# Windowed attention and squared-ReLU MLP on one core: the planner's load costs, pacing, Q turns of batch 0 and idle matmuls

## The chip, the cores and the metric

The kernel runs on one core of a Trainium2 chip. Time is device microseconds from start to end of one execution; the figure compared is the median of several runs. A profile of one execution gives every instruction's start and length on the engines: TensorE (PE, with its weight loads as PEld), VectorE (DVE), ScalarE (ACT), GpSimd (POOL) and SyncE (SP). The last two mainly issue DMAs here.

## The reference

```python
# q, k, v: 8 batches, 8 heads, 576 positions, 64 wide; w_in: 512 x 2048, w_out: 2048 x 512
scores = (1.0 / np.sqrt(D)) * np.matmul(q, k.transpose(0, 1, 3, 2))
mask = np.abs(pos[:, None] - pos[None, :]) <= 32
scores = np.where(mask, scores, -1000000000.0)
attn = softmax(scores)                       # over the last axis
x = np.matmul(attn, v).transpose(0, 2, 1, 3).reshape(B * S, H * D)     # 4608 x 512
r = np.maximum(x @ w_in, 0.0)
out = (r * r) @ w_out                        # 4608 x 512, float32
```

Each query sees at most 32 keys on either side. Nearly all arithmetic is in the two dense products.

## The kernel before, in words

**Attention.** A batch is 9 chunks of 64 queries, in all 72 chunks, numbered n. For a chunk, `scores` multiplies 128 keys with 64 queries for the 8 heads (line 565), ScalarE takes the exponential (581), VectorE multiplies with the band mask (588), `av` multiplies with V extended by a column of ones (607, 608), VectorE takes the reciprocal of that column (619) and scales into `xr` (621). `xturn` turns xr into the layout that the dense part needs, `XT`: for chunks below 18 on TensorE with a copy by ScalarE (643, 648), after that by a transposing DMA on SP's queue (631). From batch 2 on (`FB = 2`) three chunks are done together.

**Inputs.** Q, K and V are loaded in pieces by POOL's DMA queue, cast to bf16 on the way (`tok_load`, 452; `vx_load`, 514); only the first two pieces of Q and K of batch 0 come by the queues of SP and ACT (445). Q and K have to be turned: in batches 0 and 1 on TensorE (`tok_turn`, 475), with copies out of PSUM by VectorE (489), or, for Q of the first three pieces, by ScalarE (486); from batch 2 on by transposing DMAs on SP (`dma_turn`, 508). V is needed a second time shifted by 64 rows for odd chunks: VectorE copies it (`vd_half`, 524).

**Dense part.** A tile T is 512 rows of x, so 9 tiles. The first product (W1) of a tile is 16 blocks: four accumulating 128x512 products into one of two PSUM banks `HT` (`mm1`, 700), Relu by ScalarE (706), square by VectorE (715). Tile 0 and half of tile 1 use blocks of 128 rows by four (`mm1_small`, 661), called (group of rows, quarter of w_in) below; the rest of tile 1 uses `mm1_half` (682). The second product (`mm2`, 751) accumulates 16 products for 128 rows of output in one of two banks `OUTP`, then ScalarE copies the result (760) and issues its store (762). w_in and w_out are loaded once, in four quarters each, on POOL's queue (529, 534).

**Order.** The program is not written in the order in which it runs. Every operation is recorded with `rec` together with what it reads and writes, an estimated duration (`dur`) and, for DMAs, an estimate `move`: packets, ns for each, and a further latency. `schedule` plans all engines with these estimates: it plays the program forward with several pads added to each DMA's end (`PADS`), backward to find due times, and forward again with those as priorities; turns and attention (`att`) can be given a margin (`MARGINS`). Each plan's order is judged with random lateness, and the best order is kept. The order on each engine is then fixed and each engine goes through its list, waiting on semaphores where needed. So an engine's queue is strictly in order: what stands behind a waiting instruction waits too.

**Pace.** Loads of batches 2 and later are not issued as early as buffers allow. `pace` makes each load wait for a W1 block, counted in the order in which blocks are recorded:

```python
l = 2 * (9 * b + 1.8 * x + 0.6 * z - PACE)
return [("mo", max(0, int(l)))] if l < 16 * NT else []
```

where b is the batch, x the piece, and z 0, 1 or 2 for K, Q or V.

**Idle matmuls.** `fill` puts products of zeros (`ZZ`, line 405) into the planned gaps of TensorE up to a planned time `WARM` and to the operation `idle_end`, at full density up to the planned time `COLD` and at the density `SPARSE` after it. They write bank `OUTP[1]`.

Of the kernel before, what the change touches and what calls it, by code (L numbers as in the profile page):

```python
# [8 lines left out]
BF16 = mybir.dt.bfloat16  # L9
# [10 lines left out]
VS = D_ + 2  # L20
KW = 32 + S_ + 32
LEAD = 12
WARM, COLD, SPARSE = 36000, 6500, 0.5
NPE = 18
TOFF, TST = 6, 0.9
FB = 2
PACE = 15
ENGS = ("PE", "ACT", "DVE", "POOL", "SP")
PADS, MARGINS, ROUNDS, NREP = (0, 1000, 2000, 4000), (0, 4000, 10000), 3, 3
LATE = {"POOL": 1500, "SP": 2000, "ACT": 2000}  # L30
DEPTH, POST, BACK = 4000, {"POOL": 1500, "SP": 1000, "ACT": 1000}, {"POOL": 2500, "SP": 4000, "ACT": 4000}
ORDER = ("v00 v01 k02 q02 v02 w10 k03 q03 v03 w11 k04 q04 v04 w12 w13 w20 w21 w22 w23 k05 q05 "
# [7 lines left out]

class Op:
    __slots__ = ("eng", "fn", "deps", "order", "inc", "val", "sem", "dma", "dur", "key", "i",
                 "succ", "pred", "start", "end", "lat", "move", "att")


class Prog:
# [13 lines left out]
    def rec(self, eng, fn, reads=(), writes=(), dma=None, dur=100, key=0.0, move=0, old=(), att=False):  # L60
        op = Op()
        op.eng, op.fn, op.dma, op.dur, op.key, op.move = eng, fn, dma, dur, key, move
        op.att = att
        op.deps, op.order = set(), set()
        op.inc, op.val, op.sem = False, None, None
        op.lat = self.LAT[eng]
        for r in reads:
            for w in self.writer.get(r, ()):
                op.deps.add(w)
        for t in writes:  # L70
            for w in self.writer.get(t, ()):
                (op.order if w.eng == eng and w.dma is None and dma is None else op.deps).add(w)
            for r in self.readers.get(t, ()):
                (op.order if r.eng == eng and eng not in ("ACT", "DVE") and r.dma is None else op.deps).add(r)
        for t in old:
            for r in self.readers.get(t, ()):
                (op.order if r.eng == eng and r.dma is None and dma is None else op.deps).add(r)
        for r in reads:
            self.readers.setdefault(r, []).append(op)
        for t in writes:  # L80
            self.writer[t] = [op]
            self.readers[t] = []
        op.i = len(self.ops)
        self.ops.append(op)
        return op
# [10 lines left out]
    def forward(self, key=None, seq=None, rnd=None, pad=0):  # L96
# [29 lines left out]
        def serve(until):  # L126
            nonlocal now, ahead
            while now < until:
# [28 lines left out]
                if sw:  # L157
                    ahead -= x
                if op is not None:
                    end[op.i] = max(now, start[op.i] + op.dur) + POST[op.eng] + (op.move[2] if len(op.move) > 2 else 0) + (rnd.random() * rnd.late[op.eng] if rnd else pad)  # L160
                    done(op, end[op.i])
                    return True
            return False
# [99 lines left out]
    def schedule(self):  # L263
# [22 lines left out]
        for pad in PADS:  # L286
            f = self.forward(key=key, pad=pad)
            keep(f[2], f[0], f[1], f[3], ("keys", pad))
            for margin in MARGINS:
                start, T = f[0], f[3]  # L290
                for k in range(ROUNDS):
                    R = self.backward(start, T)
                    kk = [1e4 * op.key if op.key <= -100 else r - (margin if op.att else 0) for r, op in zip(R, self.ops)]
                    start, end, out, T = self.forward(key=kk, pad=pad)
                    keep(out, start, end, T, (pad, margin, k))
        self.log, self.R = log, R
# [7 lines left out]
    def fill(self, out):  # L304
        at = 1200
        for op in sorted((o for o in out if o.eng == "PE"), key=lambda o: o.start):
            gap = min(op.start, WARM, self.idle_end.start) - at
            one = 215 if at < COLD else 110
            for k in range(int((gap - 100) * (1 if at < COLD else SPARSE) // one)):
                w = Op()  # L310
                w.eng, w.fn, w.dma, w.deps, w.i = "PE", self.idle, None, {self.idle_on}, op.i
                w.inc, w.val, w.sem, w.start, w.end, w.dur, w.key = False, None, None, at + one * k, 0, one, -99
                out.append(w)
            at = max(at, op.start + op.dur)
        self.ops = sorted(out, key=lambda o: (o.start, o.i))
# [41 lines left out]
class Gen:  # L357
# [43 lines left out]
    def setup_idle(self):  # L401

        self.ms("DVE", ["zz"], self.ZZ[:], 0.0, -1000, 200)
        self.p.idle_on = self.p.ops[-1]
        self.p.idle = lambda e: e.matmul(self.OUTP[1][:, 0:256], self.ZZ[:, 0:128], self.ZZ[:, 0:256], start=True, stop=True)

    def setup_masks(self, key):
        self.p.rec("POOL", lambda e: e.iota(self.IOTA[:], [[1, 256]], base=0, channel_multiplier=-1), writes=["iota"],
# [31 lines left out]
    def first_load(self, t, x, eng, key):  # L440
        t0, n = PIECE0[x]
        src = (self.q if t == "q" else self.k)[0, :, t0:t0 + n, :].rearrange("h p d -> p h d")
        stg, tag = self.STG[t, x]
        dst = bass.AP(stg, 0, [[512, n], [64, 8], [1, 64]])
        self.p.rec(eng, lambda e: e.dma_start(dst, src), writes=[tag], dma=(f"s{t}{x}", 0), key=key, dur=420, move=(n // 2, 14, 1300))

    def tok_load(self, b, t, x, key):
        t0, n = self.pieces(b)[x]
# [3 lines left out]
        self.p.rec("POOL", lambda e: e.dma_start(dst, src), writes=[("fraw", b, t, x)], old=[("fraw", b - 2, t, y + (b == 2))],  # L452
                   reads=self.pace(b, x, "kqv".index(t)), dma=(f"f{b % 2}{t}{y}", b), key=key,
                   dur=500 + 3.2 * n, move=(n // 2, 13.3, 700 if b == 0 else 200))

    def tok_turn(self, b, x, key):
        t0, n = self.pieces(b)[x]
# [6 lines left out]
        elif b or x == 5:  # L464
            parts = [("k", "sD", self.TRP[:, 0:512]), ("q", "sD", self.TRP[:, 512:1024])]
        else:
            o = self.OUTP[0][:].bitcast(BF16)
            parts = [("k", ("outp", 0), o[:, 0:512]), ("q", ("outp", 0), o[:, 512:1024])]

        def f(e, todo):  # L470
            for t, tag, ps in todo:
# [6 lines left out]
        for todo in ([parts[:1], parts[1:]] if early else [parts]):  # L478
            rd = [self.STG[t, x][1] for t, _, _ in todo] + [("oe", 3)] if first else [("fraw", b, t, x) for t, _, _ in todo]
            self.p.rec("PE", lambda e, a=todo: f(e, a), reads=rd + ["id"],  # L480
                       writes=list({tag for _, tag, _ in todo}), key=key, dur=8 * n if first else 240 * len(todo), att=True)
        for t, tag, ps in parts:
            src = ps[:, 0:512].rearrange("p (j q) -> p j q", j=4)[:, :, 0:n]
            dst = self.KT[b % 2][:, :, 32 + t0:32 + t0 + n] if t == "k" else self.QT[b % 2][:, :, t0:t0 + n]
            if early and t == "q":
                self.p.rec("ACT", lambda e, d=dst, c=src: e.activation(d, c, ACTF.Copy), reads=[tag], writes=[(t, b % 2, x)],
                           old=self.was(b, t, x), key=key, dur=200 + 2.8 * n, att=True)
            else:
# [14 lines left out]
    def dma_turn(self, b, t, x, key):  # L503
# [3 lines left out]
        dst = self.KT[i][:, :, 32 + t0:32 + t0 + n] if t == "k" else self.QT[i][:, :, t0:t0 + n]  # L507
        self.p.rec("SP", lambda e: e.dma_start(dst, src, transpose=True), reads=[("fraw", b, t, x)], writes=[(t, i, x)],
                   old=self.was(b, t, x), dma=(f"t{t}{i}{x}", b), key=key, dur=1250, move=(32, 28 if n > 64 else 20), att=True)

    def vx_load(self, b, s, key):
        t0, n = PIECE[s]
        r = 32 if s == 0 else 0
        self.p.rec("POOL", lambda e: e.dma_start(  # L514
            self.VX[b % 2][r:r + n, s, :, 0:64], self.v[b, :, t0:t0 + n, :].rearrange("h p d -> p h d")),
            writes=[("vxl", b % 2, s), ("vxl", b % 2, s, 1)], reads=self.pace(b, s, 2), dma=(f"vf{b % 2}{s}", b), key=key, dur=500 + 3.2 * n, move=(n // 2, 13.3, 700 if b == 0 else 200))

    def vd_half(self, b, s0, s1, key):
        vd, vx = self.VD[b % 2], self.VX[b % 2]
# [219 lines left out]
    def mm2(self, T, u, seg, key):  # L739
# [9 lines left out]
        def f(e):  # L749
            for d in range(4 * seg, 4 * seg + 4):  # L750
# [2 lines left out]

        self.p.rec("PE", f, reads=[("gt", T % 2, d, u) for d in range(4 * seg, 4 * seg + 4)] + [("w2", seg)],
                   writes=[tag], key=key, dur=854)
        if x == 1 and seg == 0:
            self.p.idle_end = self.p.ops[-1]
        if seg == 3:
            oe = self.OE[x % 4]
            self.p.rec("ACT", lambda e: e.activation(oe[:], op, ACTF.Copy), reads=[tag],  # L760
# [132 lines left out]
```

## Time and profile before

| | |
|---|---|
| median of 5 runs | 311.48 us (311.04 to 312.07) |
| profiled execution | 313.03 us |
| span of its instructions | 311.2 us |
| granted TensorE clock, mean | 0.994 |
| PE busy | 298.3 us, 2801 instructions |
| first mm2 starts | 36.86 us |
| last product ends | about 308.6 us |
| DMA moved | 39.20 MB |

The span runs from the first to the last instruction; the profiled execution has 1.83 us more around it. Busy time of TensorE includes the idle matmuls, and the ends of products are modelled because they overlap: in the dense part a 128x512 product is listed with 379 ns, but four of them follow each other in 864 ns, which is the figure for sums. In a list of waits, a line reads: engine, what waited, then what it waited for, total microseconds, times, and the longest. In a timeline the columns are start, length, engine, line, operation, what is written and read, shape and count; a bracket gives the idle time of the engine ahead of it and what ended that.

### The profile page before, as it was taken

Reading aid. Unit: us, or ns where it says so; the run is one execution under the profiler, and the core shown is the slowest. Engines: PE = TensorE matmul, PEld = TensorE weight load, DVE = VectorE, ACT = ScalarE, POOL = GpSimd, SP = SyncE. Lnnn points to the kernel's source line nnn. Section 1 sums busy time; section 2 is a strip of 40 time slices with the busy share of each in tenths; the row PEclk is TensorE's granted clock in tenths of the full one; section 3 lists DMA queues with packets and bytes.
Section 4 is the critical chain, followed back from the end, with each engine's and each line's share of the span. In section 5 each row is a group of like instructions: output and inputs, shape, how many; then the busy total and the mean of one; then the engine's idle time right before and its main releaser. Section 6 shows DMA issues by size and latency. Waiting matters only on the chain.

```text
span 311.2 us, 7048 instructions
## 1 busy us (share of the span) xinstructions
PE 298.3 (96%) x2801; PEld 166.4 (53%) x2801; DVE 149.3 (48%) x449; ACT 150.3 (48%) x267; POOL 105.4 (34%) x131
## 2 busy tenths in 40 slices
PE   6969999999999999999999999999899999999996
PEld 4658845687754455444545554545354454444444
DVE  6765434664665564744556642745254542222200
ACT  2536533555746554654465544635355533434411
POOL 8999370322505533532442353333421000000000
PEclk9899999999999999999999999999999999999999
DMA  9999999994999999999999999999999420100022
GB/s 132 180 191 207 178 174 175 158 146 97 132 156 123 145 127 166 121 158 130 130 170 154 112 108 202 139 99 147 132 150 137 61 60 34 36 34 35 36 81 87
DMA packets 166098, 39.20 MB, mean 126 GB/s; under 512 B 157233, under 2 KB 161585, under 8 KB 166065
## 3 DMA queue, kind: packets, MB, share of 16 engines
q0 software_dynamic: 114144, 18.03, 90.4%
q1 hardware_dynamic: 45424, 11.09, 25.9%
q10 hardware_dynamic: 6496, 9.64, 9.5%
q8 instruction: 22, 0.36, 0.5%
q14 instruction: 12, 0.09, 0.1%
HBM read 36.70 MB, written 9.44 MB: 148 GB/s over the span
## 4 chain that ended last, share of the span: by engine, by line
PE 77%; DMA 15%; POOL 4%; DVE 1%; issue 1%; ACT 1%; SPq 0%; DVEq 0%; POOLq 0%; ACTq 0%
PE outp L751 31%; PE ht L700 28%; PE ht L661 6%; DMA vx<-in_v_dram 5%; DMA w<-in_moe_w_in_dram 3%; PE sc L565 3%; PE ht L682 2%; PE sc L607 2%; PE sc L608 2%; DMA qt<-qraw 2%; DMA kraw<-in_k_dram 2%; POOL vx L514 2%; DMA xt<-xr 1%; DMA kt<-kraw 1%; POOL qraw L452 1%
## 5 line engine op out<-in xcount | busy, mean ns | idle before, releaser
L751 PE MATMUL outp<-w,gt 128*128 128x512 bf16 x528 | 128.8, 379 | 0.0
L700 PE MATMUL ht<-xt,w 128*128 128x512 bf16 x448 | 110.2, 379 | 0.8 <-DMA xt<-xr 0.8
L706 ACT ACTIVATE rt<-ht 128x512 bf16<-128x512 f32 x112 | 66.8, 599 | 78.9 <-PE ht L700 75.3
L715 DVE TENSOR_TENSOR gt<-rt 128x512 bf16<-128x512 bf16 x144 | 60.8, 422 | 87.4 <-ACT rt L706 76.8
L751 PEld LDWEIGHTS outp<-w,gt 128*128 128x128 bf16 x528 | 49.5, 98 | 55.7
L700 PEld LDWEIGHTS ht<-xt,w 128*128 128x128 bf16 x448 | 41.8, 98 | 48.2 <-DMA xt<-xr 0.9
L452 POOL DMA_DIRECT2D kraw<-in_k_dram x39 | 33.1, 848 | 46.7 <-PE ht L700 18.2
L452 POOL DMA_DIRECT2D qraw<-in_q_dram x39 | 33.0, 847 | 45.9 <-PE ht L700 23.1
L581 ACT ACTIVATE e<-sc 128x512 bf16<-128x512 f32 x72 | 38.7, 600 | 17.6 <-PE sc L565 17.5
L514 POOL DMA_DIRECT2D vx<-in_v_dram x40 | 34.1, 853 | 36.7 <-PE ht L700 14.7
L588 DVE TENSOR_TENSOR pt<-e,mask 128x512 bf16<-128x512 bf16 x72 | 27.2, 421 | 25.1 <-ACT e L581 24.9
L760 ACT ACTIVATE oe<-outp 128x512 f32<-128x512 f32 x33 | 19.8, 599 | 23.9 <-PE outp L751 23.9
L621 DVE TENSOR_TENSOR xr<-sc,rs 128x256 bf16<-128x256 f32 x72 | 28.9, 416 | 1.0
L661 PE MATMUL ht<-xt,w 128*128 128x128 bf16 x384 | 23.8, 219 | 1.7 <-DMA w<-in_moe_w_in_dram 1.7
L524 DVE COPY vd<-vx 64x1056 bf16<-64x1056 bf16 (+1 forms) x36 | 17.5, 486 | 14.7 <-DMA vx<-in_v_dram 13.8
L661 PEld LDWEIGHTS ht<-xt,w 128*128 128x128 bf16 x384 | 21.7, 98 | 2.2 <-DMA w<-in_moe_w_in_dram 2.0
L667 ACT ACTIVATE rt<-ht 128x512 bf16<-128x512 f32 x24 | 14.4, 599 | 14.5 <-PE ht L661 14.4
L619 DVE RECIPROCAL rs<-sc 128x4 f32<-128x4 f32 x72 | 12.6, 179 | 14.6 <-PE sc L608 13.6
L565 PEld LDWEIGHTS sc<-qt,kt 64*128 64x128 bf16 x576 | 10.4, 95 | 11.7 <-issue 7.7
L565 PE MATMUL sc<-qt,kt 64*128 64x64 bf16 x576 | 13.9, 192 | 2.7 <-DMA qt<-qraw 1.6
L607 PE MATMUL sc<-vx,pt 128*128 128x65 bf16 x160 | 15.3, 194 | 0.6 <-DVE pt L588 0.4
L608 PE MATMUL sc<-vx,pt 128*128 128x65 bf16 x160 | 15.2, 194 | 0.0
(69 smaller groups left out, 163.0 us busy)
## 6 DMA issues: line engine op xcount, KB each, us to landing
out_dram<-oe ACTq DMA_DIRECT2D x35, 256.0 KB, 2.8
kraw<-in_k_dram POOLq DMA_DIRECT2D x30, 128.0 KB, 5.8
qraw<-in_q_dram POOLq DMA_DIRECT2D x30, 128.0 KB, 5.2
vx<-in_v_dram POOLq DMA_DIRECT2D x24, 128.0 KB, 5.1
w<-in_moe_w_in_dram POOLq DMA_DIRECT2D x4, 512.0 KB, 10.3
w<-in_moe_w_out_dram POOLq DMA_DIRECT2D x4, 512.0 KB, 17.5
vx<-in_v_dram POOLq DMA_DIRECT2D x16, 96.0 KB, 5.3
kt<-kraw SPq DMA_TRANSPOSE x30, 4.6
```

The source lines that it names most:

```text
L452: self.p.rec("POOL", lambda e: e.dma_start(dst, src), writes=[("fraw", b, t, x)], old=[("fraw", b - 2, t, y + (b == 2))], reads=self.pace( ...
L514: self.p.rec("POOL", lambda e: e.dma_start(self.VX[b % 2][r:r + n, s, :, 0:64], self.v[b, :, t0:t0 + n, :].rearrange("h p d -> p h d")), w ...
L565: mm = e.matmul(sc[:, o + 64 * j:o + 64 * j + 64], kt[r, j, at:at + 128], qt[r, j, at:at + 64], start=True, stop=True)
L581: self.p.rec("ACT", lambda e, d=dst, a=src: e.activation(d, a, ACTF.Exp, scale=0.125), reads=["s" + x for x in name], writes=[("e", g, x) ...
L588: self.p.rec("DVE", lambda e, a=pt, c=ee, d=mb: e.tensor_tensor(a, c, d, ALU.mult), reads=rd + ["mask"], writes=[("pt", (n + k) % 3)], key ...
L607: e.matmul(o, pt[:, a:a + 128], vt[:, ha, 0:VE], start=True, stop=False)
L621: self.p.rec("DVE", lambda e: e.tensor_tensor(bass.AP(xr, 256 * k, [[768, 128], [64, 4], [1, 64]]), bass.AP(self.SC, base, [[2048, 128], [ ...
L661: mm = e.matmul(ht[:, 128 * (d % 4):128 * (d % 4) + 128], self.W1[:, ft, 128 * d:128 * d + 128], self.XT[:, t0 // 64:t0 // 64 + 2, ft, :], ...
L700: mm = e.matmul(ht[:], self.W1[:, ft, 128 * d:128 * d + 128], self.XT[:, 8 * T:8 * T + 8, ft, :], start=(ft == 0), stop=(ft == 3))
L706: self.p.rec("ACT", lambda e: e.activation(rt[:], ht[:], ACTF.Relu), reads=[("ht", k % 2)], writes=[("rt", k % 4)], key=key, dur=560)
L715: self.p.rec("DVE", lambda e: e.tensor_tensor(g, r, r, ALU.mult), reads=[("rt", k % 4)], writes=tags, key=key, dur=430)
L751: mm = e.matmul(op, gt[:, d, 128 * u:128 * u + 128], self.W2[:, d, :], start=(d == 0), stop=(d == 15))
```

## The change

Five things change.

1. The planner's estimates. Latencies of the early loads are larger (`first_load` 1300 becomes 1400, and 2100 for the second piece; V of batch 0 700 becomes 1500, 1100 or 800). A `slack` of 3000 ns is added, in planning only, to the end of each load and each DMA turn of Q and K from batch 2 on. The pad of 4000 and the margin of 10000 are replaced by 2000 as the largest pad and 8000 as the largest margin, margins are given only to operations with a key above `LATER = 4`, and plans are judged on 4 draws instead of 3. The plan kept before was one with a pad of 2000; the plan kept now has a pad and a margin of 0.
2. `PACE` goes from 15 to 17, so each paced load waits for a W1 block that stands four earlier.
3. In batch 0, pieces 3 and 4, K is turned in `OUTP[0]` and Q in `OUTP[1]` instead of both in `OUTP[0]`, and the Q copy out of PSUM goes from VectorE to ScalarE. `idle_end` is now the turn of piece 3, because the idle matmuls write `OUTP[1]`.
4. Idle matmuls have 128 columns instead of 256, are planned at 107 ns (before `COLD`, which goes from 6500 to 9000) or 54 ns instead of 215 or 110, and fill gaps from 60 ns instead of 100.
5. A list made from a set becomes a sorted list.

Because the planner fixes the order of all engines, every engine's order changes, not only the lines named. In the built program, idle matmuls go from 37 in nine places to 56 in six (29, 2, 4, 7, 13, 1), the last of them behind the AV of chunk 2. POOL's first 39 instructions keep their order.

```diff
-WARM, COLD, SPARSE = 36000, 6500, 0.5
+WARM, COLD, SPARSE = 36000, 9000, 0.5
...
-PACE = 15
+PACE = 17
 ENGS = ("PE", "ACT", "DVE", "POOL", "SP")
-PADS, MARGINS, ROUNDS, NREP = (0, 1000, 2000, 4000), (0, 4000, 10000), 3, 3
+LATER, SLACK = 4, 3000
+PADS, MARGINS, ROUNDS, NREP = (0, 1000, 2000), (0, 4000, 8000), 3, 4
...
-        op.att = att
+        op.att, op.slack = att, 0
...
-                    end[op.i] = max(now, start[op.i] + op.dur) + POST[op.eng] + (op.move[2] if len(op.move) > 2 else 0) + (rnd.random() * rnd.late[op.eng] if rnd else pad)
+                    end[op.i] = max(now, start[op.i] + op.dur) + POST[op.eng] + (op.move[2] if len(op.move) > 2 else 0) + (rnd.random() * rnd.late[op.eng] if rnd else pad + op.slack)
...
-                    kk = [1e4 * op.key if op.key <= -100 else r - (margin if op.att else 0) for r, op in zip(R, self.ops)]
+                    kk = [1e4 * op.key if op.key <= -100 else r - (margin if op.att and op.key > LATER else 0) for r, op in zip(R, self.ops)]
...
-            one = 215 if at < COLD else 110
-            for k in range(int((gap - 100) * (1 if at < COLD else SPARSE) // one)):
+            one = 107 if at < COLD else 54
+            for k in range(int((gap - 60) * (1 if at < COLD else SPARSE) // one)):
...
-        self.p.idle = lambda e: e.matmul(self.OUTP[1][:, 0:256], self.ZZ[:, 0:128], self.ZZ[:, 0:256], start=True, stop=True)
+        self.p.idle = lambda e: e.matmul(self.OUTP[1][:, 0:128], self.ZZ[:, 0:128], self.ZZ[:, 0:128], start=True, stop=True)
...
-        self.p.rec(eng, lambda e: e.dma_start(dst, src), writes=[tag], dma=(f"s{t}{x}", 0), key=key, dur=420, move=(n // 2, 14, 1300))
+        self.p.rec(eng, lambda e: e.dma_start(dst, src), writes=[tag], dma=(f"s{t}{x}", 0), key=key, dur=420, move=(n // 2, 14, 1400 + 700 * x))
...
+        self.p.ops[-1].slack = SLACK if b >= FB else 0
...
-            o = self.OUTP[0][:].bitcast(BF16)
-            parts = [("k", ("outp", 0), o[:, 0:512]), ("q", ("outp", 0), o[:, 512:1024])]
+            parts = [(t, ("outp", u), self.OUTP[u][:].bitcast(BF16)) for u, t in enumerate("kq")]
...
-                       writes=list({tag for _, tag, _ in todo}), key=key, dur=8 * n if first else 240 * len(todo), att=True)
+                       writes=sorted({tag for _, tag, _ in todo}), key=key, dur=8 * n if first else 240 * len(todo), att=True)
+        if b == 0 and x == 3:
+            self.p.idle_end = self.p.ops[-1]
...
-            if early and t == "q":
+            if b == 0 and x < 5 and t == "q":
...
+        self.p.ops[-1].slack = SLACK
...
-            writes=[("vxl", b % 2, s), ("vxl", b % 2, s, 1)], reads=self.pace(b, s, 2), dma=(f"vf{b % 2}{s}", b), key=key, dur=500 + 3.2 * n, move=(n // 2, 13.3, 700 if b == 0 else 200))
+            writes=[("vxl", b % 2, s), ("vxl", b % 2, s, 1)], reads=self.pace(b, s, 2), dma=(f"vf{b % 2}{s}", b), key=key,
+                   dur=500 + 3.2 * n, move=(n // 2, 13.3, (1500, 1100, 800, 800, 800)[s] if b == 0 else 200))
+        self.p.ops[-1].slack = SLACK if b >= FB else 0
...
-        if x == 1 and seg == 0:
-            self.p.idle_end = self.p.ops[-1]
```

The three added `slack` lines stand at the end of `tok_load`, `dma_turn` and `vx_load`, in this order.

## The prediction

> **What bounds the kernel now.** I read the page first: busy shares, then the 40 slices.
>
> ```profile
> PE 298.3 (96%) x2801; PEld 166.4 (53%) x2801; DVE 149.3 (48%) x449; ACT 150.3 (48%) x267; POOL 105.4 (34%) x131
> ...
> PE   6969999999999999999999999999899999999996
> ...
> PEclk9899999999999999999999999999999999999999
> ```
>
> TensorE is at 96%, nearly everywhere at nine tenths; the thin slices are the first three or four (0 to about 25 us) and one near 220 us. The change removes no product, so it can gain only where TensorE does nothing of use: those stretches, and its idle matmuls (L405), which count as busy. The table by stretches (columns: stretch, its length, then busy us and count of PE, PEld, DVE, ACT, POOL, granted clock, DMA share, GB/s) puts a number on the start:
>
> ```profile
> 15.00:19.20 4.20, 1.89 (x34) 1.24 (x32) 3.20 (x9) 1.78 (x4) 4.20 (x7) 1.00 1.83 180
> 19.20:25.40 6.20, 5.52 (x99) 4.67 (x99) 3.99 (x12) 3.37 (x6) 6.20 (x8) 1.00 1.30 205
> ```
>
> Then TensorE's waits, first those after 28.8 us, where no idle matmul is left:
>
> ```profile
> PE sc L565 <- DMA qt<-qraw: 1.6, 1, 1.6
> PE sc L643 <- DVE xr L621: 1.0, 2, 0.7
> PE ht L700 <- DMA xt<-xr: 0.8, 1, 0.8
> PE sc L565 <- DMA kt<-kraw: 0.3, 1, 0.3
> ```
>
> That is 3.65 us in five waits (0.34 and 0.70 make the second line), which is all that a better steady schedule can win. For the start, the timeline of TensorE:
>
> ```profile
> 15.10 0.82 PE L405 MATMUL outp<-zz 128*128 128x256 bf16 x6
> 16.55 0.41 PE L565 MATMUL sc<-qt,kt 64*128 64x64 bf16 x16 [0.64 <-DVE qt L489]
> ...
> 19.18 1.07 PE L661 MATMUL ht<-xt,w 128*128 128x128 bf16 x16 [1.67 <-DMA w<-in_moe_w_in_dram]
> ...
> 23.28 0.41 PE L565 MATMUL sc<-qt,kt 64*128 64x64 bf16 x16
> ...
> 24.25 0.71 PE L405 MATMUL outp<-zz 128*128 128x256 bf16 x5
> ```
>
> At 19.18 everything stands on the second quarter of w_in: issued at 9.24, landed 9.9 us later. The built order of POOL's first 39 instructions is unchanged and none of them waits for TensorE, so this landing is an anchor: what is saved before it is lost again.
>
> **Start, after the anchor.** Before, TensorE does W1 block (group 0, quarter 1), AV 4, block (1,0), the turn of piece 4 at 21.22, AV 5, block (1,1), scores 6 at 23.28, then idle matmuls until AV 6 at 25.39; from there 11.47 us of dense work lead to the first mm2 at 36.86 (28.8 is only where the long run of blocks begins). In the changed order block (1,0) stands before the anchor and (1,1) takes its place before the turn; so the turn stays at 21.22, and after AV 6 the same twelve blocks follow. The gain is what AV 6 moves. The copies after the turn decide:
>
> ```profile
> 21.42 0.60 ACT L667 ACTIVATE rt<-ht 128x512 bf16<-128x512 f32 x1 [0.54 <-PE ht L661]
> 21.71 0.73 DVE L524 COPY vd<-vx 64x528 bf16<-64x528 bf16 x1
> 22.47 0.42 DVE L489 COPY kt<-outp 128x512 bf16<-128x512 bf16 x1
> 22.81 0.41 DVE L489 COPY qt<-outp 128x512 bf16<-128x512 bf16 x1
> ```
>
> VectorE copies K, then Q, until 23.22. Now ScalarE copies Q after the Relu: 22.02 + 0.60 (its own 128x512 Q copy took 597 ns) = 22.62, and K, with the same VectorE work ahead, ends at about 22.8. Scores start near 22.83, so AV 6 and all behind it come 0.45 us earlier. Bounds: 0 if K's copy slips by 0.45; 0.9, one block, if block (1,0) ahead of the anchor counted in full. The next weight quarters landed at 23.4 and 26.3, W2 at 28.7 to 36.3; 0.45 us earlier meets none.
>
> **Idle matmuls.** 37 of 256 columns become 56 of 128, none after piece 3's turn (14 stood there). At full clock six took (0.82-0.28)/5 = 0.108 each, so the new ones some 0.055, or 0.1 cold. The 13 ahead of the second X turn cost at most 13 x 0.1 = 1.3 us; block (1,0) should end near 17.4, so the 1.7 us before 19.15 covers that. Without this cover it is up to 1.3. Here a rule speaks against the change. Row: with 8 idle matmuls, 15.0 to 19.2 had PE busy 1.89 of 4.2 at clock 1.00. The Trainium skill (TensorE: Matmul & The Clock Gate, "Why this matters for your kernels") wants no idle gap over about 3 us, else the clock halves. Afterwards I count 0.2 + 0.35 + 0.9 = 1.45 us busy there (X turn, scores, block), in pieces, longest gap 1.75: by the row nothing, by the rule's limit also nothing, but if such thin work counts as idle, one 3.4 us stretch at half speed costs 1.7. I take 0 and keep 1.7.
>
> **Two waits behind VectorE's V copies.** The X turns of chunk 8 and of chunks 10 and 11 wait 0.34 and 0.70, since xr stood behind a vd copy waiting for V:
>
> ```profile
> 58.62 0.43 DVE L524 COPY vd<-vx 64x1056 bf16<-64x1056 bf16 x1 [1.57 <-DMA vx<-in_v_dram]
> ...
> 60.00 0.40 PE L643 MATMUL sc<-identw,xr 128*128 128x128 bf16 x4 [0.70 <-DVE xr L621]
> ```
>
> In the new VectorE order both xr stand ahead of that copy, and V of batch 2, piece 0, is issued ahead of K and Q of piece 1, no longer behind them. Gain 0.34 + 0.70 = 1.04; bounds 0.4 (a half of each comes back at the next copy, less what is hidden) to 1.04.
>
> **Loads and turns of batches 2 to 7.** PACE 17 frees each load four W1 blocks earlier, about 7 us at 0.86 us for a block and 0.86 for the mm2 between. But the plan, made with slack, also brings attention forward. I summed TensorE work (0.864 per four 512-column products, 0.52 per triple of scores, 0.25 per AV) between the end of the block that frees a load and the scores that read it. Before, the two sites that waited had 11.1 us (K piece 3, chunks 39 to 41: wait 0.27) and 12.8 (Q piece 1, chunks 63 to 65: wait 1.57), so the way from gate to scores takes 11.4 to 14.4. In the long one the X turn of chunk 60 stood ahead of the Q turn on SP:
>
> ```profile
> 218.40 1.28 SPq L631 DMA_TRANSPOSE xt<-xr  x1
> 219.77 1.22 SPq L508 DMA_TRANSPOSE qt<-qraw  x1
> ```
>
> and the landing took 6.15 us after 219.77, where 4.4 is the median of Q turns. In the new order the smallest distance is 13.4 and that Q turn stands ahead of the X turn, so it needs about 14.4-1.4 = 13.0 with the long landing and 11.3 with the median. Both waits go: 0.27 + 1.57 = 1.84; bounds 0.8 (one us remains at the second) to 1.84. VectorE's V copies also stand 4.2 to 7.4 us behind their gates, before mostly 2.2 to 5.
>
> **A wait that grows.** W1 of tile 2 needs the X turn of chunks 21 to 23. AV 23 ended at 87.6, the turn was issued at 88.90, landed after 4.58, and TensorE went on at 93.53: 5.9 us, against 4.7 us of work between. The new plan starts from no pad on X turns (before, 2 us on every DMA), and AV 25 and 26 moved behind the first block, so 4.2 us of work stand there. The wait rises by 0.5, to about 1.3. Later tiles have 7.4 us or more. What waits behind it is all of TensorE. Bounds 0.5 to 2 (if the turn lands in 6.15).
>
> **Sum.** -0.45 - 1.04 - 1.84 + 0.5 = -2.83; for small new waits of an order that no trace shows I allow 0.25 (0 to 1): -2.6. The profiled execution took 313.03, its span 311.2; after it 310.4 and 308.6. Against the median of 311.48, 1.55 below the profiled one, it is **308.9 us**. This case's own range is 308.0 to 310.4: all gains at their best and nothing new give -0.9 - 1.04 - 1.84 + 0.5 = -3.3, and the weakest single end, the grown wait at 2, leaves -1.1; some 0.2 of scatter is added below.
>
> **Rivals.** (A) The clock halves once in the thin start: 308.9 + 1.7 = 310.6. For: the clock was 0.72 between 5 and 10.4 us, after a wait of 1.5; against: 1.00 later over equal gaps. Chance 0.12. (B) Supply and demand move together: attention of chunk 45 comes 12 us earlier in TensorE's work while its loads come 7, and if the way takes 15 us, the eight sites with 13.4 to 14.3 wait again, giving back some 2.3: 311.2, no change. Against it is the measured 11.4. Chance 0.08. (C) Slower: on SP the X turn of chunks 21 to 23 now stands behind the K and Q turns of batch 3, piece 2; before, it stood ahead of them, and that Q load was issued only at 94.98. SP waits in order, so a late Q load holds tile 2 and with it TensorE. Its gate now ends near 78.5; plus 5.3 landing and 1.2 issue is 85.1, and xr is ready near 87.3: 2.2 us to spare. From 2.2 + 2.6 + 0.6 = 5.4 us late the kernel is slower; 8 us late gives 308.9 + 5.8 = 314.7. For: POOL also waits in order, and stood 10.9 us once before. Against: all gates ahead of it come earlier too. Chance 0.12.
>
> **Chances.** Forecast 0.68, A 0.12, B 0.08, C 0.12. Faster by over 0.2% (what a measurement here can tell from no change): forecast and A, 0.80; within: 0.08; slower: 0.12. The range 307.7 to 311.3 takes in the forecast, A and B, with scatter at both ends, and leaves out C.
>
> **What would show it.** No Q or K wait of TensorE over 0.5 us behind 60 us; no wait for xr near 48 and 60; the wait for xt at the first L700 product (now behind shifted lines) at 1.3; first mm2 near 36.4; clock 1.00 from 15 on. Wrong it would be by a clock below 1 between 15 and 28, by a wait of several us near 92, or if the first mm2 comes no earlier, since then the start does not hang on the Q copy.

## The result, and the profile after

The changed kernel takes 310.67 us (median of 44 runs, 308.72 to 313.64); the kernel before, beside it, 311.82 (79 runs, 309.87 to 316.0). The ratio is 0.996, 95% interval 0.9948 to 0.9972: faster by 0.4%, 1.2 us. The forecast was 308.9, 2.6 us faster. The time lies in the forecast range, the direction is right, and the gain is a little under half of what was forecast (0.4% against 0.8%). How the parts of the sum came out is another matter: the runs below show that the gain was made at the place where the forecast booked a loss, and that two of its three gains were not there.

The profiled execution of the changed kernel took 309.99 us, its span 308.2. That is 3.0 us less than the profiled one before, but the medians differ by 1.2: the execution profiled before was 1.2 us slower than its median, this one is 0.7 us faster than its own. Keep this in mind wherever a term was read from one trace.

The page of the changed kernel, its busy shares and slices:

```profile
PE 297.4 (97%) x2820; PEld 168.4 (55%) x2820; DVE 148.2 (48%) x447; ACT 149.9 (49%) x269; POOL 105.3 (34%) x131
...
PE   7979999989989999999999999999999999999996
...
PEclk9799999999999999999999999999999999999999
```

The thin slice near 220 us is gone, and two eights stand at 62 to 70 and 85 to 92 us. TensorE's waits after 28.8 us, in the answer limited to that stretch (columns: who waits for whom, us in all, times, longest):

```profile
PE sc L613 <- DVE pt L594: 1.5, 1, 1.5
PE ht L706 <- DMA xt<-xr: 0.8, 1, 0.8
PE sc L571 <- DVE qt L492: 0.7, 1, 0.7
```

None of the waits for K or Q turns and none for xr is left, as forecast. But 3.0 us of waits stand there against 3.65 before: 2.2 of them are new, both behind VectorE, and the wait for the X turn of tile 2 (L706) did not grow. The timeline of TensorE shows where:

```profile
42.42 0.29 PE L571 MATMUL sc<-qt,kt 64*128 64x64 bf16 x8 [0.71 <-DVE qt L492]
...
67.78 0.20 PE L613 MATMUL sc<-vd,pt 128*128 128x65 bf16 x1 [1.51 <-DVE pt L594]
...
92.28 1.02 PE L706 MATMUL ht<-xt,w 128*128 128x512 bf16 x4 [0.81 <-DMA xt<-xr]
```

VectorE's timeline at the first two shows what it was doing:

```profile
41.49 0.62 DVE L530 COPY vd<-vx 64x1056 bf16<-64x1056 bf16 x1 [5.13 <-DMA vx<-in_v_dram]
42.03 0.20 DVE L492 COPY kt<-sc 128x128 bf16<-128x128 bf16 x1
42.16 0.20 DVE L492 COPY qt<-sc 128x128 bf16<-128x128 bf16 x1
...
66.56 0.43 DVE L530 COPY vd<-vx 64x1056 bf16<-64x1056 bf16 x1 [2.87 <-DMA vx<-in_v_dram]
67.29 0.42 DVE L594 TENSOR_TENSOR pt<-e,mask 128x512 bf16<-128x512 bf16 x1
```

It stood for 5.13 and 2.87 us on a V load, with the Q copy and the mask that TensorE needed queued behind the V copy. The V load of the second site (batch 2, piece 3) was issued at 46.72 and landed 19.8 us later, at 66.5. GpSimd's six V loads between 38 and 70 us took (minimum, median, maximum):

```profile
DMA to landing us min/median/max: 9.2/13.9/19.8
```

By the Trainium skill (DMA: Bandwidth & Descriptors, "Anatomy of one DMA — SWDGE (gpsimd) path") a single such transfer costs 2.0 us and its bytes at 436 GB/s, by estimate 2.3 us for 128 KB. The measured values are those of a queue with a backlog (the 16 DMA engines were busy nine tenths or more in every slice of this stretch), and they decide.

The start, TensorE first, then the copies on ScalarE and VectorE, in three answers of the timeline:

```profile
17.25 1.96 PE L667 MATMUL ht<-xt,w 128*128 128x128 bf16 x32 [0.35 <-ACT xt L654]
...
20.18 0.39 PE L476 MATMUL outp<-identw,kraw 128*128 128x128 bf16 x4
...
21.52 0.41 PE L571 MATMUL sc<-qt,kt 64*128 64x64 bf16 x16 [0.49 <-ACT qt L489]
...
23.63 0.20 PE L613 MATMUL sc<-vx,pt 128*128 128x65 bf16 x1 [1.19 <-DVE pt L594]
```

```profile
20.88 0.59 ACT L489 ACTIVATE qt<-outp 128x512 bf16<-128x512 bf16 x1
```

```profile
20.83 0.43 DVE L492 COPY kt<-outp 128x512 bf16<-128x512 bf16 x1
```

K and Q are now copied side by side. From the turn of piece 4 to scores 6 it is 1.34 us, before 2.06. The first mm2 stands at 35.11, before at 36.86: 0.72 from the copies, and the rest because the second quarter of w_in landed at 18.0 in this execution, 1.1 us earlier than in the one before, so that nothing waited for it. So the anchor itself moves from execution to execution: in the other fifteen traces the landing lies between 18.0 and 18.8.

### The profile page after: what moved, and what is told of

Read it like the earlier page. It is cut to its first block, busy times and chain, and to the rows that moved or that the text cites. A ratio compares the mean times of both kernels' runs of the same rounds, so it can differ in the third digit from the quotient of the medians.

```text
span 308.2 us, 7090 instructions
## 1 busy us (share of the span) xinstructions
PE 297.4 (97%) x2820; PEld 168.4 (55%) x2820; DVE 148.2 (48%) x447; ACT 149.9 (49%) x269; POOL 105.3 (34%) x131
## 4 chain that ended last, share of the span: by engine, by line
PE 82%; DMA 9%; POOL 4%; DVE 2%; issue 2%; ACT 1%; POOLq 0%
PE outp L757 33%; PE ht L706 32%; DMA vx<-in_v_dram 6%; PE ht L667 4%; PE sc L571 3%; PE sc L613 3%; PE sc L614 3%; PE ht L688 2%; DMA qraw<-in_q_dram 2%; POOL vx L518 1%; POOL kraw L453 1%; DMA xt<-xr 1%; POOL qraw L453 1%; PE outp L406 1%; PE sc L731 1%
## 5 line engine op out<-in xcount | busy, mean ns | idle before, releaser
L757 PE MATMUL outp<-w,gt 128*128 128x512 bf16 x528 | 131.8, 379 | 0.0
L706 PE MATMUL ht<-xt,w 128*128 128x512 bf16 x448 | 112.9, 379 | 0.8 <-DMA xt<-xr 0.8
L706 PEld LDWEIGHTS ht<-xt,w 128*128 128x128 bf16 x448 | 41.5, 98 | 47.1 <-issue 0.9
L453 POOL DMA_DIRECT2D kraw<-in_k_dram x39 | 33.1, 850 | 44.4 <-PE ht L706 18.8
L530 DVE COPY vd<-vx 64x1056 bf16<-64x1056 bf16 (+1 forms) x36 | 16.0, 446 | 12.6 <-DMA vx<-in_v_dram 11.7
```

Of the source, the lines that this page charges most:

```text
L706: mm = e.matmul(ht[:], self.W1[:, ft, 128 * d:128 * d + 128], self.XT[:, 8 * T:8 * T + 8, ft, :], start=(ft == 0), stop=(ft == 3))
L757: mm = e.matmul(op, gt[:, d, 128 * u:128 * u + 128], self.W2[:, d, :], start=(d == 0), stop=(d == 15))
```

## Experiments

Every time is the median of its runs, with the ratio to the kernel before in the same session and its 95% interval. Where traces are compared, one account holds for all seventeen: from the start of tile 2 (its first 128x512 product of W1) to the end it takes 215.7 to 216.1 us, once TensorE's waits behind that start, and 1.6 us of half clock in b_again, are taken off. So a trace is told by when tile 2 starts and by what TensorE waits for after it; how the waits ahead of tile 2 trade with the start is the question of the runs. Waits under 0.17 us, and those at places where the record of a product is missing from the trace, are left out. Names with b_ are the kernel before with an edit or again, those with a_ the changed kernel; p15_ is planned anew.

| trace | median us | ratio, 95% | span | first mm2 | tile 2 | waits behind the first mm2: at about us |
|---|---|---|---|---|---|---|
| before | 311.82 |  | 311.2 | 36.86 | 93.53 | 3.65: xr 48, 60; xt 93; K 136; Q 226 |
| b_again | 312.51 | 0.9998 (0.996–1.0036) | 311.3 | 36.25 | 94.02 | 2.99: xr 48, 59; xt 94 (1.92), and 1.6 of half clock |
| b_look | 311.73 (one run) |  | 309.9 | 37.19 | 93.86 | 2.48: xr 48, 60; xt 94; 0.35 at 108 |
| b_gate17 | 310.85 | 0.996 (0.9934–0.9986) | 309.1 | 36.45 | 92.49 | 2.18: xr 48, 60; Q 192 |
| b_gate_late | 312.24 | 1.0003 (0.9975–1.0031) | 310.7 | 36.47 | 93.94 | 3.42: xr 48, 60; xt 94 (1.74); Q 194 |
| b_gate_early | 310.69 | 0.9943 (0.9914–0.9971) | 308.3 | 36.27 | 92.40 | 1.33: xr 49; 0.19 at 45 |
| b_xr | 312.98 | 0.9998 (0.9965–1.0031) | 310.2 | 36.57 | 93.57 | 3.30: Q copy 46; xr 62; xt 94; K 137 |
| after | 310.67 | 0.996 (0.9948–0.9972) | 308.2 | 35.11 | 92.28 | 3.03: Q copy 42; mask 68; xt 92 |
| a_again | 310.66 | 0.9939 (0.9914–0.9963) | 308.5 | 38.37 | 92.41 | 0.53: mask 69 |
| a_again2 | 310.81 | 0.998 (0.9947–1.0012) | 307.2 | 35.95 | 91.26 | 1.57: mask 68 |
| a_vd | 309.11 | 0.9906 (0.9868–0.9943) | 308.0 | 35.62 | 91.98 | 2.34: xr 46, 64; xt 92 |
| a_gate15b2 | 312.04 | 0.9972 (0.9938–1.0006) | 312.2 | 36.12 | 96.28 | 4.68: mask 70 (4.24); xt 96 |
| a_qdve | 310.87 | 0.9962 (0.9933–0.9991) | 310.2 | 40.01 | 94.14 | 0.42: xt 94 |
| a_noidle | 313.55 | 1.0059 (1.0019–1.0099) | 309.1 | 38.13 | 93.06 | 1.04: mask 69; xt 93 |
| a_idle16 | 310.37 | 0.9949 (0.9922–0.9975) | 308.7 | 35.96 | 92.70 | 2.84: xr 64; mask 69 |
| a_pace15 | 308.66 | 0.9895 (0.985–0.994) | 306.9 | 35.53 | 90.81 | 1.22: mask 64; 0.17 at 167 |
| p15_all | 308.0 | 0.9868 (0.9828–0.9907) | 305.6 | 35.83 | 89.84 | none |

### Both kernels traced again

No edit.

> The kernel before, unchanged, profiled a second time. Theory S (the waits of the first profile belong to the schedule): TensorE again waits about 1.6 us for a Q turn near 226 us, 0.3 for a K turn near 136, 0.3 and 0.7 for xr near 48 and 60; first mm2 near 36.9; ratio 1. Theory R (most of them are chance in the landing of one execution's DMAs): the Q wait is below 0.5 us or elsewhere, the second quarter of w_in lands up to 1 us away from 19.1, and the span differs by more than 0.5 us from 311.2.

> The changed kernel, unchanged, profiled a second time. Theory S: first mm2 near 35.1, a wait of 0.7 us for the Q copy of piece 5 near 42 and of 1.5 us for a masked tile near 67.8, both behind a V copy of VectorE; ratio 0.996. Theory R: the second quarter of w_in lands nearer 19.1, first mm2 at 36.0 to 36.5 (only the 0.45 to 0.7 us of the Q copy are the change's), and the wait near 42 shrinks by as much as the start is later; ratio 0.996 as well.

In the second trace of the kernel before, the K and Q turns at 136 and 226 us are not waited for at all. TensorE's waits behind 28.8 us there:

```profile
PE ht L700 <- DMA xt<-xr: 1.9, 1, 1.9
PE outp L751 <- issue: 1.4, 9, 0.2
PE sc L643 <- DVE xr L621: 1.1, 2, 0.6
```

(The nine of 0.2 are places where the trace lacks the record of a product: it has 2766 of them beside 2801 weight loads.) The wait for the X turn of tile 2 is 1.92 in place of 0.77. In the second trace of the changed kernel the first mm2 comes 3.3 us later than in the first, and yet the span grows by only 0.3: of the 3.0 us of waits behind it, 0.5 are left. The same is seen in other traces with this order (35.95 with 1.57 in a_again2, 40.01 with 0.42 in a_qdve). What TensorE saves or loses at the start is mostly taken back before 92 us, where it meets loads that come at their own time.

### Earlier gates alone

The order of the kernel before on every engine, but each paced load waits for a W1 block four earlier, as with PACE 17.

```diff
+NEWPACE = 17
...
+        m = l - 2 * (NEWPACE - PACE)
+        self.gated = (r[0][1], max(0, int(m))) if r else ()
...
+                op.deps = (op.deps - {self.mo[g[0]]}) | {self.mo[g[1]]}
```

> The order of before on every engine, but each paced load waits for the W1 block that PACE 17 names (four earlier); nothing is planned anew. Theory S: the waits for the K and Q turns near 136 and 226 us go, 1.84 us less, ratio 0.994. Theory R: the median execution had little of these waits, 0.3 to 0.6 us less, ratio 0.998 to 0.999.

0.996, between the two theories: in this order the gates alone give what the whole change gave. To see which of them do it, the loads of batches 4 to 7 alone (`* (b > 3)` on the step) and those of batches 2 and 3 alone (`* (b < 4)`), with a third trace of the kernel before:

> The kernel before in its own order, with the loads of batches 4 to 7 alone freed four W1 blocks earlier. Theory P (the prediction's term: the waits for a K turn near 136 us and a Q turn near 226 us, 0.27 and 1.57 in the profiled execution, are a cost of every execution, and earlier gates remove them): 1.84 of 312, ratio 0.993 to 0.995, and no such wait in its trace. Theory S (those waits were those of one execution; in a second trace of the same kernel neither was there, so most executions do not pay them): no such wait either, but a ratio of 0.998 to 1.001.

> The same with the loads of batches 2 and 3 alone freed four W1 blocks earlier, the others as before. Theory P: these gates only have V and the turns for the first tiles ready sooner, no wait that the prediction counted is behind them: ratio 0.999 to 1.001. Theory S (what the earlier gates won, 0.4% when all were moved, they won at the X turn that tile 2 waits for, whose transfer then does not share the DMA engines with these loads): ratio 0.995 to 0.998, tile 2 begins at 92.2 to 93 us in place of 93.5 to 94.0, with no wait for xt over 0.5 us and no half clock behind it.

> The kernel before, unchanged, for a third trace of it. By theory P the Q turn near 226 us is waited for 1.6 us again, and the K turn 0.3 us; by theory S neither reaches 0.5 us.

The late gates give nothing, 1.0003. The early ones give as much as all of them, 0.9943. Five traces have the late gates of before (before, b_again, b_look, b_xr, b_gate_early): the Q turn near 226 us is waited for in one of them, and the K turn near 136 in two (0.27 and 0.75). The term of 1.84 us was a wait of one execution. Nor do earlier late gates keep such waits away: the profile names no cause for the 0.61 us at 194 in b_gate_late and the 0.82 at 192 in b_gate17, but both end 0.09 us after a Q turn has landed, 7.6 and 7.8 us after its issue.

Where the early gates earn their time is tile 2. The timeline of TensorE with the late gates moved:

```profile
93.94 1.90 PE L717 MATMUL ht<-xt,w 128*128 128x512 bf16 x8 [1.74 <-DMA xt<-xr]
```

and with the early ones:

```profile
92.40 1.90 PE L717 MATMUL ht<-xt,w 128*128 128x512 bf16 x8
```

The X turn was issued at the same time, 88.33 and 88.49. The DMA view of 86 to 92 us (queue, packets, MB, share of 16 engines; and below it the issue with its us to landing), late gates moved:

```profile
q0 software_dynamic: 1765, 0.22, 61.5%
...
xt<-xr SPq DMA_TRANSPOSE x1, 5.6
```

and early gates moved:

```profile
q0 software_dynamic: 691, 0.09, 22.6%
...
xt<-xr SPq DMA_TRANSPOSE x1, 3.9
```

With the gates of before, GpSimd's loads (q0) move more packets here, and the turn takes 1.7 us longer. But 1494 of the 1765 packets fall between 86 and 88 us, before this turn is issued. What runs beside them is the turn ahead of it in SP's queue, a Q turn. Late gates moved, then early gates moved:

```profile
85.69 1.33 SPq L524 DMA_TRANSPOSE qt<-qraw  x1
88.33 2.43 SPq L648 DMA_TRANSPOSE xt<-xr  x1
```

```profile
85.49 1.26 SPq L524 DMA_TRANSPOSE qt<-qraw  x1
88.49 1.21 SPq L648 DMA_TRANSPOSE xt<-xr  x1
```

The Q turn lands at 92.45 in the first and at 90.72 in the second, and the X turn 1.4 and 1.6 us after it. The other five traces of this order agree. The X turn lands 1.3 to 2.0 us after that Q turn, and tile 2 starts 0.04 to 0.05 us after the X turn. Where batches 2 and 3 have the gates of before (before, b_again, b_look, b_gate_late, b_xr), there are 1512 to 2062 packets of loads in these 6 us, and the X turn lands between 93.5 and 94.0, whether it was issued at 88.2 or at 89.1. With the early gates moved (b_gate_early, b_gate17) there are 691 and 844, and it lands at 92.4. So tile 2 hangs on a landing that, in these traces, came no sooner when the X turn was issued sooner, but did when the loads were. That the loads hold up the Q turn by sharing the 16 DMA engines fits these numbers; no run separates it from another cause. The changed kernel has 591 such packets and lands the turn at 92.14.

### The two V copies ahead of xr

The kernel before, with the two V copies that held up xr near 48 and 60 us moved behind it on VectorE, nothing else.

```diff
+MOVES = ((95, 98), (112, 115))
...
+        dve = [o for o in self.ops if o.eng == "DVE"]
+        for a, b in MOVES:
+            self.ops.remove(dve[a])
+            self.ops.insert(self.ops.index(dve[b]) + 1, dve[a])
```

> The order of before, but on VectorE two V copies (batch 1, second half, first part; batch 2, first half, first part) are moved behind the xr of chunk 8 and of chunk 11. Theory S: the waits for xr near 48 and 60 us go, 1.04 us less, ratio 0.9967. Theory R: what is behind the moved copies waits in its place (the masked tile of chunk 9, the K copy of piece 3), 0 to 0.4 us less, ratio 0.9987 to 1.

Both waits are gone from the trace, and the time is the same, 0.9998. TensorE's waits behind 28.8 us in it:

```profile
PE ht L705 <- DMA xt<-xr: 1.4, 1, 1.4
PE sc L612 <- DVE xr L626: 0.8, 1, 0.8
PE sc L570 <- DMA kt<-kraw: 0.7, 1, 0.7
PE sc L570 <- DVE qt L494: 0.4, 1, 0.4
```

What was won at 48 and 60 us is waited for at 46, 62 and 94: the X turn of tile 2 is issued at 88.32 and lands at 93.52, no earlier than in the other traces with these gates. So the 1.04 us of the sum was not to be had while these gates stood.

### The new waits in the changed order

The changed kernel with two V copies moved behind the Q copy and the masks: `MOVES = ((86, 89), (125, 138))`, with the same lines as above.

> The changed kernel with two V copies of VectorE moved back in its order: the first of batch 1 behind the mask of chunk 8, the first of batch 2's second half to just ahead of its partner. Theory S: the waits of 0.7 near 42 and 1.5 near 67 us go, 2.2 us less, ratio 0.987 to 0.989. Theory L: they go, but tile 2 waits for its X turn instead (1 to 2 us in the profile) or a later load; tile 2 not before 91.3; 0 to 1 us less, ratio 0.991 to 0.996.

0.9906, where the unchanged kernel has 0.996 in its 44 runs and 0.9939 and 0.998 in the others: the two new waits are worth some 0.3 to 0.7%, though a part returns at 64 us (1.32 for xr) and at the X turn of tile 2 (0.76), as theory L said. Is it the order or the earlier loads of batch 2 that make them? The changed order, with the gates of batch 2 alone put back by four W1 blocks:

```diff
+        m = l - 2 * (NEWPACE - PACE) * (b == 2)
```

> The changed kernel's order, with the gates of the loads of batch 2 alone put back by four W1 blocks (the kernel before's distance). Theory G (the earlier gates crowd the DMA engines, which carry a backlog until about 66 us, and so delay the loads that VectorE stands on near 42 and 67 us): both waits, 0.71 and 1.51, shrink by half or more, and the time comes near that of the schedule planned anew with the old gates: ratio 0.990 to 0.993. Theory O (the waits come from VectorE's order, in which the V copies stand ahead of masks and Q copies that TensorE needs): V of batch 2, piece 3 lands at 66.5 to 67.5 all the same, the wait near 67.8 stays or grows by up to 1 us, and the ratio is 0.995 to 0.999.

The ratio, 0.9972, is theory O's, and the wait grew further than it said, to 4.24 us (the traced execution took 314.0, 2.0 over the median, so this is at the upper end). VectorE and TensorE at this place:

```profile
69.28 0.43 DVE L549 COPY vd<-vx 64x1056 bf16<-64x1056 bf16 x1 [5.60 <-DMA vx<-in_v_dram]
```

```profile
70.49 0.20 PE L632 MATMUL sc<-vd,pt 128*128 128x65 bf16 x1 [4.24 <-DVE pt L613]
```

The V load was issued at 58.62, 11.9 us later than in the changed kernel, and VectorE's copy began 2.7 us later: the load landed in 10.6 us here and in 19.8 there. So the earlier gates do not crowd these loads out (theory G is wrong). In this pair of traces they help, by about a quarter of their head start. The plan placed the V copy too near to the landing and the mask behind it.

### The start

Q copies of pieces 3 and 4 back on VectorE, behind the K copy, the rest as in the changed kernel:

```diff
+        for q, k, fn in self.back:
+            q.eng, q.fn = "DVE", fn
+            self.ops.remove(q)
+            self.ops.insert(self.ops.index(k) + 1, q)
```

> The changed kernel with the Q copies of pieces 3 and 4 back on VectorE, right behind the K copy. Theory S: scores of chunks 6 and 7, and with them the first mm2 and the end, come 0.3 to 0.7 us later than in the changed kernel, ratio 0.997 against 0.995. Theory L: first mm2 later by that, tile 2 and the end not, ratio as for the changed kernel.

Scores 6 wait 1.24 us for the Q copy in place of 0.49, and the time is 0.9962, the same as the changed kernel's 0.996. No worth of the ScalarE copy can be measured, though an interval of 0.3% to each side could not show 0.45 us (0.14%). The first mm2 at 40.01 in this trace is not due to the copy alone: the granted clock was 0.80 from 26 to 28 us, 0.50 from 28 to 30 and 0.85 from 30 to 32.

Without any idle matmul (`WARM = 0`):

> The changed kernel without any idle matmul. Theory S (each microsecond saved at the start is saved at the end): the clock is half in more of the first 25 us, the first mm2 comes 1 to 3 us later than 35.1, and the kernel is that much slower than the changed one: 312 to 313.5 us, ratio 1.000 to 1.005. Theory L (up to tile 2, near 92 us, the loads set the time, and TensorE's start only trades its waits): first mm2 later by as much, tile 2 still between 92 and 93, ratio 0.994 to 0.997 as for the changed kernel.

1.0059, a little beyond theory S and 1.0% slower than the changed kernel (313.55 to 310.67). Its trace is of the fastest of its twelve runs (310.88). The first W1 block in it:

```profile
15.90 1.90 PE L667 MATMUL ht<-xt,w 128*128 128x128 bf16 x16
```

It takes 1.90 us; with idle matmuls ahead it took 1.07 at 14.13. The profile's clock row shows 1.00 there, so here the durations tell the clock. In this run tile 2 still starts at 93.06. Where the others lose 2.7 us more no trace shows; that a start still later is no longer taken back is likely and not shown.

The changed kernel has no idle matmul after the turn of piece 3. In a_again the clock halved there. Windows of 2 us from 24 to 30 (columns as in the prediction's table by stretches):

```profile
24.00:26.00 2.00, 0.94 (x18) 0.97 (x19) 1.23 (x4) 0.94 (x2) 2.00 (x3) 0.91 1.24 205
26.00:28.00 2.00, 2.00 (x26) 2.00 (x24) 0.73 (x4) 0.60 (x1) 2.00 (x3) 0.50 1.24 206
28.00:30.00 2.00, 2.00 (x29) 2.00 (x28) 0.64 (x3) 0.60 (x1) 2.00 (x4) 0.74 1.24 206
```

So 16 idle matmuls were put back ahead of AV 6, into columns 256 to 383 of the bank, which the Q turn does not use:

```diff
+MORE = 16
...
+            extra = MORE if pe.index(op) == pe.index(self.idle_at) + 2 else 0
+            for k in range(max(extra, int((gap - 60) * (1 if at < COLD else SPARSE) // one))):
...
+        self.p.idle = lambda e: e.matmul(self.OUTP[1][:, 256:384], self.ZZ[:, 0:128], self.ZZ[:, 0:128], start=True, stop=True)
```

> The changed kernel, with 16 idle matmuls of 128 columns put back between the X turn that follows scores 6 and AV 6, where it waited 1.1 to 1.2 us with 0.8 us of work in the 2.6 us before, and where the kernel before had 5 idle ones of 256 columns. In two of the five profiles of kernels with this start the clock halved just after this place (0.50 to 0.91 in some windows of 24 to 30 us) and the first mm2 came at 38.4 or 40.0 and not at 35.1 to 35.6. Theory C (the removed idle matmuls are what lets the clock fall there): clock 1.00 from 16 us on, first mm2 at 35 to 36.2, and a lower median than the changed kernel by up to 0.8 us (2 in 5 times 2 us), 309.9 to 310.4. Theory L (what is lost before about 92 us is absorbed, since tile 2 then stands on loads): clock 1.00 as well, but the time within 0.2% of the changed kernel's.

> The changed kernel once more, as it is, beside the others: 310.7 (ratio 0.994 to 0.996). It gives one more profile of the start: by theory C a clock below 1 in 24 to 30 us with a chance of about 2 in 5.

The clock stays at 1.00, but a_again2 shows 1.00 there too, without them. Of six traces of this order with no idle matmuls ahead of AV 6 (after, a_again, a_again2, a_vd, a_gate15b2, a_qdve), two halve there. The mean clock of every run says more: it is 0.983 or 0.984 in 16 of the changed kernel's 67 runs, 0.983 in the traced one of a_again, and below 0.989 in none of the 18 runs of a_idle16 and p15_all, which have these idle matmuls. So they seem to keep the clock up, as theory C says, while the time hardly follows: those 16 runs have a median of 310.87 us, the other 51 of 310.66. With 310.37 beside 310.81, ratios 0.9949 and 0.998 and overlapping intervals, whether the 16 idle matmuls save any time stays open.

### A plan with slack and the old gates

The changed kernel with `PACE = 15`, planned anew: slack, Q turns and idle matmuls as in the change.

> The changed kernel with PACE back at 15 and planned anew, so all orders differ a little. If the earlier loads are what makes the kernel faster: ratio 0.998 to 1.004, with waits of TensorE for Q or K turns or for the X turn of tile 2 of 1 us or more. If the plan with slack is: ratio 0.994 to 0.997.

0.9895, better than with 17 and than either theory had it, so the gain does not need the earlier gates once the plan is made anew. One wait of note is left, 1.05 at 64 us, again a mask behind V copies. With those two copies moved behind the masks (`MOVES = ((122, 125), (123, 122))`) and the 16 idle matmuls:

> The schedule planned anew with the old gates (308.66, ratio 0.9895), with the 16 idle matmuls at AV 6, and with the two V copies of batch 2 that held AV back near 64 us moved behind the two masks: the version that the experiments point to. If gains before tile 2 add: less 1.05 and less the clock's share, 307.0 to 307.8 (ratio 0.984 to 0.987). If they are absorbed by the wait for the loads that tile 2 stands on: 308.4 to 308.9 (ratio 0.989 to 0.990).

308.0 us, 0.9868, as if the gains add (six runs, as for a_pace15): faster than both kernels, by 0.9% over the changed one. TensorE's waits behind 28.8 us, all that is left, and these are missing records:

```profile
PE outp L767 <- issue: 0.5, 3, 0.2
PE sc L767 <- issue: 0.2, 1, 0.2
```

Against 0.9895 the intervals overlap, so the last step is shown by its trace (no wait, tile 2 at 89.84 in place of 90.81) and not by its time. Both issue the X turn of tile 2 sooner, at 86.53 and 85.56 (the changed kernel at 88.2 to 89.4 in its three traces), and it lands at 90.67 and 89.54. Why the planner finds a better order with the old gates, while in the order of before the new gates are better, stays open.

## Why the prediction was right or wrong

The step that failed is the reading of waits: 2.88 of the 3.33 us of gain were waits of TensorE in one trace, each booked as time that the whole kernel would save. The runs put two things in its place. The late waits (1.84) are not paid by most executions. The early ones (1.04) come back in each trace of the kernel before, but what is saved there is waited for again at the X turn of tile 2, whose landing moves with the loads of batches 2 and 3. At that landing the gain was made, and there the forecast had booked a loss.

**Start, -0.45.** The mechanism was as told: scores 6 wait for ScalarE's Q copy, 0.72 us sooner behind the turn (0.45 was forecast), and from AV 6 to the first mm2 it took 11.48 us as forecast (11.47). That this gain reaches the end is not shown: in a_again 3.3 us at the start became 0.3 at the end, and a_qdve cannot tell so small a term.

**Idle matmuls, 0, with 1.7 for rival A.** The half-clock stretch came in one trace of three of the changed kernel and, by the mean clocks, perhaps in 16 of 67 runs, oftener than the 0.12 given. But it cost little there, some 0.2 us of the median in place of 1.7, for the same reason. The rule on idle gaps that was weighed in the prediction (the Trainium skill, TensorE: Matmul & The Clock Gate, "Why this matters for your kernels") did not foretell it: the gap ahead of it was 1.13 us, in a stretch of 2.6 us with 0.8 busy. So a thin stretch was followed by half clock in some executions, as was feared, and in others not.

**Two waits behind V copies, -1.04, and 0.25 for new small waits.** This step is wrong. The waits are places where TensorE meets the V loads of batches 1 and 2, which landed only after 9.2 to 19.8 us in the changed kernel; b_xr strikes the waits out and wins nothing, since the X turn of tile 2 lands no sooner. In the changed kernel V loads of the same two batches stopped TensorE at 42 and 67 us for 2.2, 0.5 and 1.6 us in its three traces, where 0.25 was allowed. The sentence on V copies that stand 4.2 to 7.4 us behind their gates was the right place to look, but it measured the distance in TensorE's work, and did not ask how long the landing took.

**Loads and turns of batches 2 to 7, -1.84.** The waits are gone, as forecast, but they were not a cost of the kernel: b_gate_late gives 1.0003. The step that failed is the first one, taking a wait of 1.57 from one trace as a cost of each execution. That the profiled execution was 1.55 us slower than the median was on the page, and was carried along as an offset instead of being asked whether the wait was that offset.

**A wait that grows, +0.5.** The sign is wrong. The work between AV 23 and tile 2 did shrink, from 5.1 to 4.5 us, but the term took the turn's 4.58 us of landing as fixed. It follows the Q turn ahead of it, which runs beside GpSimd's loads, and with the earlier gates these loads were further on: 3.9, 2.8 and 2.7 us of landing in the three traces of the changed kernel and waits of 0.81, 0 and 0. Tile 2 starts at 92.3, 92.4 and 91.3 there, at 93.5, 94.0 and 93.9 in the three of the kernel before. In the order of before b_gate_early (0.9943) shows this to be the gain; that it is the same in the changed order is read from these traces.

**Rivals.** B had a true core: waits for loads came back. But they came back at V copies, not at K and Q turns, of which TensorE waited for none. C did not come: SP issued the X turn at 88.27, 0.6 us earlier than before. Its place was the right one to look at, an X turn behind K and Q turns on SP's queue.

That the direction came out right is in good part luck, then: -0.45 and -1.04 were mostly absorbed, -1.84 was not there, and the 1.2 us were won at tile 2, where +0.5 was booked.

## What to carry to other kernels

On a kernel that waits for a few us in all, take a second and third trace before a wait goes into a sum: a wait that one execution shows may be the very reason why it was slower than the median. A wait of the bounding engine ahead of a place where it meets a load need not be won by removing it; follow it to the next meeting and count only what the load itself comes earlier. When transfers are issued earlier, ask not only who waits for them but which other transfer on the critical chain then runs with less beside it, and what stands behind that one in its queue.

## What the runs showed of the hardware

A wait of 1.92 us for the X turn in b_again was followed by half clock. Windows there:

```profile
92.00:94.00 2.00, 0.11 (x4) 0.00 (x0) 1.04 (x4) 0.00 (x0) 0.00 (x0) 1.00 1.24 260
94.00:96.00 2.00, 1.98 (x6) 0.77 (x7) 0.00 (x0) 0.29 (x1) 0.00 (x0) 0.57 0.64 150
96.00:98.00 2.00, 2.00 (x29) 0.84 (x28) 0.43 (x1) 0.89 (x2) 0.87 (x1) 0.57 0.11 7
```

The eight products behind it were busy for 3.36 us; in b_gate_late, behind a wait of 1.74, for 1.90, at full clock. The Trainium skill (TensorE: Matmul & The Clock Gate, "HAM oscillation — how this bites in real kernels") puts the limit at gaps of about 3.4 us. The wait of 4.24 us in a_gate15b2 agrees: the granted clock behind it was 0.91, 0.50 and 0.74 in the three windows of 2 us from 70 us on. In b_again a gap of little more than half of the limit was enough, once; waits of 0.77 to 1.74 at the same place in four other traces of this order were not. The block after the eight products starts 3.91 us behind the first of them, in b_gate_late 2.29, so the wait of 1.92 us cost 1.6 more.
